# Eight blocks of each V gradient on ScalarE, six kept V tiles, four gradient tiles

## The chip, the cores and the metric

The kernel runs on one core of one Trainium2 chip. The metric is the device time of one execution in microseconds (us). Before the change it is 903.56 us, the median of 3 runs (903.27 to 903.65). The profile is one further execution of the same program. A measurement of this kernel agrees with its repetitions to within about 0.1%.

The engines are named as in the profile: PE is TensorE (PEld its weight loads), DVE is VectorE, ACT is ScalarE, POOL is GpSimd, SP is the engine that issues the loads. GB/s is what the core's 16 DMA engines moved.

## The reference

The reference computes one decoding step of a transformer block and all its gradients. With `B = 2` batch rows, `H = 32` heads, `Sk = 4096` cached positions and `Dh = 128`:

```
def _A_ref(x, k_cache, v_cache, wq, wo):
    q = (x @ wq) by heads
    scores = einsum("bhqd,bhkd->bhqk", q, k) * (Dh ** -0.5)
    p = _softmax(scores, axis=-1)
    o = einsum("bhqk,bhkd->bhqd", p, v)
    return o @ wo
def _B_ref(x, w1, w2):
    return relu(x @ w1) @ w2

h  = x + _A_ref(_layernorm(x), k_cache, v_cache, wq, wo)
h2 = h + _B_ref(_layernorm(h), w1, w2)
_out, _vjp = jax.vjp(_f, A_x, A_k_cache, A_v_cache, A_wq, A_wo, B_w1, B_w2)
_grads = _vjp(grad_out)
```

Almost all bytes are the K and V caches and their gradients. For each pair of batch row and head there are a K and a V tile of 4096 x 128 bf16 (1024 KB each) to read and a K and a V gradient of the same size to write. Each gradient is an outer product. Row s of the V gradient is `P[s]` (the softmax weight) times the vector `go` of that head. Row s of the K gradient is `gs[s]` times the query, with `gs[s] = P[s] * (V[s] . go - dot)`. So the gradient of K needs V a second time, once `go` is known, and `go` needs the whole forward pass of its batch row.

## The kernel before, in words

**Two sweeps.** The first sweep (`p1_iter`, one pass per pair, 64 pairs in order) reads K and V, makes scores, softmax and sums, and keeps the softmax weights in `P_bf`. The second sweep (`p2_iter`, one turn j per pair) reads V again (in the second sweep a V tile is called W), multiplies it with `go` and writes both gradients. The second sweep starts while the first still runs on batch row 1, one turn for two passes. From pass 64 on there is a turn in each, and after pass 65 the second sweep runs alone, from turn 14 to turn 63.

**Kept tiles.** The V tiles of the last `KEPT[b]` heads of a batch row stay in the on-chip memory after the first sweep, and the second sweep takes these heads first (`turns`), so they are not read again. `KEPT = (6, 5)`: six of batch row 0 and five of batch row 1, thus 53 W loads for 64 turns. The kept heads of batch row 1 are turns 32 to 36.

**Tiles and their homes.** Tiles of 1024 KB come from a list of homes (`take`, `give`). There are 12 at first, 14 when the second sweep runs alone, and more at the end. A home has a tag: `ld` for loads, `g` for gradients (`gK`, `gV`), `f` and `q` for late work. `share(ld=..., g=...)` says how many homes of each tag are wanted, and `give` moves a returned home to a tag that has too few. Homes of one tag are taken in the order in which they were given back. When the second sweep runs alone, line 1147 asks for `KEPT[1] + 4 = 9` load tiles and 5 gradient tiles. From turn `H + KEPT[1] - 1 = 36` on, line 1158 shares for the late work. Loads are issued on SP in one fixed order (`queue`, `pump`), each as soon as the order of the program has given a load home back, and SP waits there until the last user of that home is done.

**A turn.** `p2_iter` is a generator of six steps (a `yield` ends each):

- step 0: the last of four rounds of L436 for the head before (V times `go`), its `gsp` on VectorE (L821), `rb` on ScalarE (L835, the rows `go` and q of this head, spread over all partitions and scaled by one number per partition), `pp` on POOL (L837), the first of four transposes of W (TensorE L423, copied to `t_sb` by ScalarE, L428), and the first half of the K gradient of the head before (L808);
- step 1: the second half of that K gradient and its store, issued on POOL (L846);
- steps 2 to 4: the other three transposes with their copies, and the L436 rounds; step 4 also returns W and makes the first half of this head's V gradient (`gV`, L808);
- step 5: the second half of `gV`, and its store, issued on POOL (L865).

A half is one VectorE instruction on 128 x 2048 elements (`outer_half`). There are no barriers between steps: each engine works through its own list of instructions and waits only for what an instruction needs. Between the steps, other work is inserted at set rates: the middle of the network (`middle_gen`, whose L644 steps make `go` in groups of heads, first a group of the kept heads), the outer products for the weight gradients (`fin_gen`, tiles `ot`), and the gradient of x (`gx_gen`).

Of the kernel before, what the change touches and what calls it, by code (L numbers as in the profile page):

```python
# [7 lines left out]
FP32 = mybir.dt.float32  # L8
BF16 = mybir.dt.bfloat16
ALU = mybir.AluOpType  # L10
# [5 lines left out]
def kernel(  # L16
# [20 lines left out]
    nc = tc.nc  # L37
# [67 lines left out]
    def give(t, to=None):  # L105
        tag, k, _ = home_of.pop(id(t))
        to = to or goes_to(tag)
        owned[tag] -= 1
        owned[to] += 1
        free[to] += 1  # L110
        homes[to].append(k)
        given_at[k] = step[0]
# [279 lines left out]

    pairs = [(b, h) for b in range(B) for h in range(H)]
    NP1 = len(pairs)
    KEPT = (6, 5)
    turns = [(b, h) for b in range(B) for h in (*range(H - KEPT[b], H), *range(H - KEPT[b]))]
    turn_of = {bh: j for j, bh in enumerate(turns)}
    kept = {(b, h) for b in range(B) for h in range(H - KEPT[b], H)}
# [404 lines left out]
    def pairs_view(t):  # L803
        return t.rearrange("p s (a two) -> p s a two", two=2)

    def outer_half(dst, row, colp, k):
        sl = slice(k * HALF, (k + 1) * HALF)
        nc.vector.tensor_tensor(  # L808
            out=pairs_view(dst[:, sl, :]),
            in0=row.rearrange("p (a two) -> p a two", two=2)[:, None, :, :].to_broadcast([128, HALF, 64, 2]),  # L810
            in1=colp[:, sl, None, :].to_broadcast([128, HALF, 64, 2]), op=ALU.mult)

    def p2_iter(j, busy):

        c = S2[j] if j < NP1 else None
        p = S2[j - 1] if j >= 1 else None
# [7 lines left out]
        if c is not None:  # L824
            b, h = turns[j]
            go = gom[:, h, b, :, :]

            bank = pst([128, 512], FP32, "sps", "dp_ps")
            for k, col in enumerate((goc, qsc)):
                nc.tensor.matmul(bank[:, 128 + k * 128:256 + k * 128],  # L830
                                 lhsT=col[:, h, b:b + 1].to_broadcast([128, 128]), rhs=ident_bf[:],
                                 start=True, stop=True)
            c["dp"] = bank[:, 0:NSC]
            rb = mats.tile([128, 256], BF16, tag="rb", bufs=4, name="rb")
            nc.scalar.activation(out=rb[:], in_=bank[:, 128:384], func=ACT.Copy, scale=rt[:, b, h:h + 1])  # L835
            pp = small.tile([128, NSC, 2], BF16, tag="pp", name="pp")
            nc.gpsimd.tensor_copy(out=pp[:], in_=P_bf[:, b * H + h, :, None].to_broadcast([128, NSC, 2]))  # L837
            c.update(rb=rb, pp=pp)
            c["T0"] = pair_transpose(c["W"], 0, busy=busy)
        if p is not None:  # L840
            gK = take("g", [128, NSC, 128], "gK")
# [2 lines left out]
        if p is not None:  # L844
            outer_half(gK, p["rb"][:, 128:256], gsp, 1)
            nc.gpsimd.dma_start(out=natural(out_2, bp, hp), in_=gK[:])  # L846
            give(gK)
            del S2[j - 1]
        yield
        if c is None:  # L850
            return
        c["T1"] = pair_transpose(c["W"], 1, busy=busy)
        pair_matvec(c["dp"], c.pop("T0"), 0, go)
        yield
        c["T2"] = pair_transpose(c["W"], 2, busy=busy)
# [5 lines left out]
        gV = take("g", [128, NSC, 128], "gV")  # L861
        outer_half(gV, c["rb"][:, 0:128], c["pp"], 0)
        yield
        outer_half(gV, c["rb"][:, 0:128], c["pp"], 1)
        nc.gpsimd.dma_start(out=natural(out_3, b, h), in_=gV[:])  # L865
        give(gV)
        yield


# [270 lines left out]
    for n, (i, j) in enumerate(plan):  # L1140
        all_go = all(("go", B - 1, h) in done for h in range(H))
        if i is None and plan[n - 1][0] is not None:
            pkp.release()
            big1 = tc.alloc_tile_pool(name="big1", bufs=1)
            for _ in range(2):
                more_home("ld", big1)
            share(ld=KEPT[1] + 4, g=5)
        if all_go and not late[0]:
            wop.release()
            big3 = tc.alloc_tile_pool(name="big3", bufs=1, side="right")  # L1150
# [8 lines left out]
        if j is not None:  # L1159
            while g2 is not None:  # L1160
                p2_step()
            if j < NP1:
                bg_until(("go", *turns[j]))
            g2 = p2_iter(j, 0)
        if i is None and ("w1", 1) in done and fin is None:
            wts.release()
            fin = tc.alloc_tile_pool(name="fin", bufs=1)
# [90 lines left out]
```

## Time and profile before

| | |
|---|---|
| median of 3 runs | 903.56 us |
| the profiled execution | 902.98 us, of which the span from the first to the last instruction is 901.1 us |
| busy: PE, DVE, ACT, POOL | 82%, 77%, 49%, 21% of the span |
| read, written | 212.16 MB, 149.13 MB |
| a half of `gV` or `gK` on VectorE (128 x 2048) | 1.22 us |
| `rb` on ScalarE (128 x 256, scale per partition) | 0.474 us |
| a `t_sb` copy on ScalarE (128 x 512) | 0.587 us |
| `pp` on POOL (most of them) | 0.25 us |
| `gV` stores, issue to landing | 14.8 us median, 4.3 to 29.1 |

The span by stage, with the mean granted clock of TensorE and the rate of the DMA:

| stage, us | what runs | clock | GB/s |
|---|---|---|---|
| 0 to 222 | first sweep, batch row 0 | 0.97 | 402 |
| 222 to 311 | middle of the network for batch row 0 | 0.98 | 343 |
| 311 to 444 | first sweep, batch row 1, with the second sweep at half rate | 0.95 | 422 |
| 444 to 622 | end of the first sweep, then the second alone, turns to 32 | 0.62 | 411 |
| 622 to 735 | turns 33 to 45 with the late work | 0.58 | 404 |
| 735 to 888 | the other turns | 0.58 | 424 |
| 888 to 901 | the last stores land | 0.50 | 249 |

In the profile's tables a line of a stretch gives, after its bounds and length, the busy time of PE, PEld, DVE, ACT and POOL with the number of instructions, then the granted clock, the DMA share and GB/s. A line of a timeline gives start, duration, engine, source line and what is written from what. A line of waits gives the total, the number of times and the longest, in us.

### The profile page before, as it was taken

To read this page: it belongs to the slowest core of one execution; us is meant where nothing else is said; L and a number is where in the kernel's file an instruction comes from. 1 tells how busy PE (TensorE), PEld (TensorE's weight loads), DVE (VectorE), ACT (ScalarE), POOL (GpSimd) and SP (SyncE) were. 2 spreads that over 40 slices of the span, in tenths; PEclk is the share of its full clock that TensorE was granted. 3 is DMA by queue.
4 is the path that set the end of the run, shared out by engine and by line. 5 is a ranking of instruction groups with operands and counts; after the bars stand their busy time and mean duration, and the time that the engine had idled before them with its cause. 6 is when DMAs were issued, how large, how long until landed. Compare 5 with 4: busy or idle time off the path is not lost.

```text
span 901.1 us, 24395 instructions
## 1 busy us (share of the span) xinstructions
PE 739.2 (82%) x10145; PEld 618.0 (69%) x10145; DVE 695.8 (77%) x1284; ACT 442.9 (49%) x1090; POOL 192.9 (21%) x330
## 2 busy tenths in 40 slices
PE   4998899899999897997877856865887799679780
PEld 4887788788888786886766845653766576466460
DVE  2665778677779886886878879978897459999972
ACT  1443334344456564564543534543665666467560
POOL 1343434343311111010011112111221111111120
PEclk9999999899999999898995556655566555575565
DMA  9999999999789999999999999999999999999997
GB/s 377 419 409 405 409 397 409 419 419 359 301 323 341 415 423 422 421 423 422 417 384 403 421 424 395 423 418 416 415 417 406 408 379 424 425 425 425 425 423 319
DMA packets 56430, 362.87 MB, mean 403 GB/s; under 512 B 5696, under 2 KB 11776, under 8 KB 15488
## 3 DMA queue, kind: packets, MB, share of 16 engines
q1 hardware_dynamic: 34664, 212.17, 58.3%
q0 software_dynamic: 18432, 134.23, 35.7%
q10 hardware_dynamic: 3224, 14.92, 4.0%
q8 instruction: 80, 1.31, 0.6%
q14 instruction: 30, 0.25, 0.1%
HBM read 212.16 MB, written 149.13 MB: 401 GB/s over the span
## 4 chain that ended last, share of the span: by engine, by line
PE 47%; DMA 25%; DVE 15%; ACT 5%; issue 5%; SPq 0%; POOL 0%; ACTq 0%; POOLq 0%; DVEq 0%
PE t_ps L423 20%; DMA Vt<-in_A_v_cache_dram 12%; PE m_ps L457 10%; DMA out_dram<-gV 7%; DVE gV L808 5%; DMA out_dram<-gK 4%; PE s_ps L436 3%; DVE gK L808 3%; PE u_ps L486 3%; ACT t_sb L428 3%; PE o_ps L902 3%; PE dp_ps L436 2%; DVE pk L464 2%; DVE junk L644 2%; DMA Kt<-in_A_k_cache_dram 2%
## 5 line engine op out<-in xcount | busy, mean ns | idle before, releaser
L428 ACT COPY t_sb<-t_ps 128x512 f32<-128x512 f32 x479 | 274.4, 587 | 212.5 <-PE t_ps L423 206.3
L436 PEld LDWEIGHTS <-t_sb 128*128 128x128 bf16 x4096 | 179.3, 102 | 43.1 <-ACT t_sb L428 21.4
L423 PE MATMUL t_ps<-ident_f,Wt 128*128 128x128 f32 x848 | 196.4, 380 | 0.2 <-ACT t_sb L428 0.2
L457 PE MATMUL m_ps<-pk,Vt 128*128 128x129 bf16 x2048 | 173.5, 224 | 18.0 <-DMA Vt<-in_A_v_cache_dram 16.0
L464 DVE TENSOR_TENSOR pk<-Kt,ep 128x2048 bf16<-128x2048 bf16 x128 | 156.5, 1223 | 30.8 <-ACT ep L512 14.1
L808 DVE TENSOR_TENSOR gK<-rb,gsp 128x2048 bf16<-128x2048 bf16 x128 | 152.5, 1225 | 17.2 <-DMA out_dram<-gV 15.2
L423 PE MATMUL t_ps<-ident_f,Kt 128*128 128x128 f32 x1024 | 156.9, 287 | 6.7 <-DMA Kt<-in_A_k_cache_dram 6.2
L808 DVE TENSOR_TENSOR gV<-rb,pp 128x2048 bf16<-128x2048 bf16 x128 | 152.9, 1219 | 10.0 <-DMA out_dram<-gK 7.9
L457 PEld LDWEIGHTS <-Vt 128*128 128x128 bf16 x2048 | 126.7, 99 | 49.2 <-issue 29.8
L423 PEld LDWEIGHTS t_ps<-ident_f,Wt 128*128 128x128 f32 x848 | 137.2, 198 | 29.3 <-issue 23.4
L423 PEld LDWEIGHTS t_ps<-ident_f,Kt 128*128 128x128 f32 x1024 | 114.0, 146 | 11.0 <-issue 5.9
L474 POOL COPY pk<-ep 128x16 bf16<-128x16 bf16 x80 | 84.8, 1062 | 166.5 <-ACT ep L512 86.8
L436 PE MATMUL dp_ps<-gom,t_sb 128*128 128x2 bf16 x2048 | 95.8, 168 | 10.9 <-ACT t_sb L428 10.4
L846 POOL DMA_DIRECT2D out_dram<-gK x64 | 34.0, 532 | 267.3 <-DVE gK L808 204.8
L865 POOL DMA_DIRECT2D out_dram<-gV x64 | 34.2, 534 | 258.1 <-DVE gV L808 202.2
L436 PE MATMUL s_ps<-qm,t_sb 128*128 128x2 bf16 x2048 | 87.7, 164 | 1.5 <-DVE t_sb L426 1.5
L908 ACT CAST ot<-o_ps 128x512 bf16<-128x512 f32 (+3 forms) x152 | 67.2, 492 | 10.7 <-DMA out_dram<-ot 9.2
L571 ACT CAST MT<-m_ps 128x128 bf16<-128x128 f32 x64 | 17.1, 267 | 107.7 <-PE m_ps L457 107.6
L821 DVE SCALAR_TENSOR_TENSOR gsp<-dp_ps,negdot,P_bf 128x64 bf16<-128x64 f32 x64 | 18.0, 281 | 52.0 <-PE dp_ps L436 51.6
L835 ACT ACTIVATE rb<-dp_ps,rt 128x256 bf16<-128x256 f32 x64 | 30.4, 475 | 56.0 <-PE dp_ps L830 55.2
L644 DVE CUSTOM_DVE_ANT_0 junk<-wo_t,hbc 128x640 bf16<-128x640 bf16 x64 | 52.4, 819 | 0.2
L644 DVE CUSTOM_DVE_ANT_0 gxj<-wqs,gqr 128x1024 bf16<-128x1024 bf16 x40 | 48.8, 1221 | 0.2
(198 smaller groups left out, 702.7 us busy)
## 6 DMA issues: line engine op xcount, KB each, us to landing
Kt<-in_A_k_cache_dram SPq DMA_DIRECT2D x64, 1024.0 KB, 15.0
Vt<-in_A_v_cache_dram SPq DMA_DIRECT2D x64, 1024.0 KB, 13.8
out_dram<-gV POOLq DMA_DIRECT2D x64, 1024.0 KB, 14.8
out_dram<-gK POOLq DMA_DIRECT2D x64, 1024.0 KB, 14.1
Wt<-in_A_v_cache_dram SPq DMA_DIRECT2D x53, 1024.0 KB, 12.5
wq_t<-in_A_wq_dram SPq DMA_DIRECT2D x5, 1024.0 KB, 6.9
wo_t<-in_A_wo_dram SPq DMA_DIRECT2D x4, 1280.0 KB
wqs<-in_A_wq_dram SPq DMA_DIRECT2D x5, 1024.0 KB, 15.8
```

Of the source, the lines that this page charges most:

```text
L423: nc.tensor.transpose(t_ps[:, j, :], natf[:, 2 * cc:2 * cc + 2, :].rearrange("p c k -> p (c k)"), ident_f[:])
L428: nc.scalar.copy(out=t_sb[:], in_=t_ps[:])
L436: nc.tensor.matmul(dst[:, sc:sc + 2], lhsT=v[:, j, :, par], rhs=vecs[:, par, :], start=(par == 0), stop=(par == 1))
L457: nc.tensor.matmul(r["m"][:, 0:129], lhsT=r["V"][:, sc, :], rhs=r["pk"][sc // HALF][:, sc % HALF, 0:129], start=(sc == 0), stop=(sc == NSC ...
L464: nc.vector.tensor_tensor(out=p["pk"][k][:, :, 0:128].rearrange("p s (a two) -> p s a two", two=2), in0=p["K"][:, sl, :].rearrange("p s (a ...
L474: nc.gpsimd.tensor_copy(out=col, in_=e)
L644: nc.vector.tensor_tensor_reduce(out=junk[0:kc, 0:width], in0=in0, in1=in1, scale=1.0, scalar=0.0, op0=ALU.mult, op1=ALU.add, accum_out=acc)
L808: nc.vector.tensor_tensor(out=pairs_view(dst[:, sl, :]), in0=row.rearrange("p (a two) -> p a two", two=2)[:, None, :, :].to_broadcast([128 ...
L835: nc.scalar.activation(out=rb[:], in_=bank[:, 128:384], func=ACT.Copy, scale=rt[:, b, h:h + 1])
L846: nc.gpsimd.dma_start(out=natural(out_2, bp, hp), in_=gK[:])
L865: nc.gpsimd.dma_start(out=natural(out_3, b, h), in_=gV[:])
L908: nc.scalar.copy(out=ot[0:P, k, n0:n0 + nn], in_=o_ps[0:P, 0:nn])
```

## The change

Three things change together.

1. `KEPT` becomes (6, 6). A sixth V tile of batch row 1 stays. There are 52 W loads; the kept heads are turns 32 to 37; the first `go` group of batch row 1 has six heads and the last has two instead of three. `share` in line 1147 asks for `KEPT[1] + 4 = 10` load tiles, and the sharing for the late work begins one turn later.
2. In that same line the gradient tiles asked for are 4, not 5.
3. In turns 14 to 32 (the second sweep alone, `j <= H`) VectorE leaves out the last eight of the 32 blocks of each `gV` (a block is 128 x 128), so its second half is 128 x 1024. ScalarE makes these eight in step 2 of the next turn, behind the copy of that turn's second transpose: each is `rb` times one number per partition. POOL copies these numbers to fp32 (`pa`) in step 0. The store of `gV` is then issued in step 2 of the next turn, on POOL behind `pp`, `pa` and the K store, and the tile is returned only there.

```diff
-    KEPT = (6, 5)
+    KEPT = (6, 6)
...
-    def outer_half(dst, row, colp, k):
-        sl = slice(k * HALF, (k + 1) * HALF)
+    def outer_half(dst, row, colp, k, short=0):
+        n = HALF - short
+        sl = slice(k * HALF, k * HALF + n)
...
-    def p2_iter(j, busy):
+    def p2_iter(j, busy, act=0):
...
+            if act:
+                pa = small.tile([128, act], FP32, tag="pa", bufs=2, name="pa")
+                nc.gpsimd.tensor_copy(out=pa[:], in_=P_bf[:, b * H + h, NSC - act:NSC])
             c["T0"] = pair_transpose(c["W"], 0, busy=busy)
...
+        yield
+        if c is not None:
+            c["T1"] = pair_transpose(c["W"], 1, busy=busy)
+        if p is not None:
+            if "gV" in p:
+                gV, pa, bp, hp, n = p["gV"]
+                for k in range(n):
+                    nc.scalar.activation(out=gV[:, NSC - n + k, :], in_=p["rb"][:, 0:128], func=ACT.Copy,
+                                         scale=pa[:, k:k + 1])
+                nc.gpsimd.dma_start(out=natural(out_3, bp, hp), in_=gV[:])
+                give(gV)
             del S2[j - 1]
...
-        outer_half(gV, c["rb"][:, 0:128], c["pp"], 1)
-        nc.gpsimd.dma_start(out=natural(out_3, b, h), in_=gV[:])
-        give(gV)
+        outer_half(gV, c["rb"][:, 0:128], c["pp"], 1, act)
+        if act:
+            c["gV"] = (gV, pa, b, h, act)
+        else:
+            nc.gpsimd.dma_start(out=natural(out_3, b, h), in_=gV[:])
+            give(gV)
...
-            share(ld=KEPT[1] + 4, g=5)
+            share(ld=KEPT[1] + 4, g=4)
...
-            g2 = p2_iter(j, 0)
+            g2 = p2_iter(j, 0, 8 if i is None and j <= H else 0)
```

## The prediction

> **What bounds the kernel now.** I read the page's slices first, then the chain, then busy time by stretch, the load queue by time, the waits of VectorE and the stores' landing times.
>
> The page's slices of the span, and its chain by engine:
>
> ```profile
> DMA  9999999999789999999999999999999999999997
> GB/s 377 419 409 405 409 397 409 419 419 359 301 323 341 415 423 422 421 423 422 417 384 403 421 424 395 423 418 416 415 417 406 408 379 424 425 425 425 425 423 319
> PE 47%; DMA 25%; DVE 15%; ACT 5%; issue 5%; SPq 0%; POOL 0%; ACTq 0%; POOLq 0%; DVEq 0%
> ```
>
> The DMA engines are full in nearly every slice, at 415 to 425 GB/s where nothing disturbs them. TensorE leads the chain, but from slice 20 (450 us) on it is the DMA that is full while the others have gaps. Busy time by stretch (PE, weight loads, DVE, ACT, POOL, granted clock, DMA share, GB/s) shows the part that the change touches:
>
> ```profile
> 444.00:454.00 10.00, 7.88 (x111) 7.04 (x110) 6.63 (x18) 4.47 (x11) 0.53 (x1) 0.83 0.96 399
> 454.00:462.00 8.00, 7.29 (x134) 6.46 (x132) 6.89 (x12) 4.02 (x13) 2.02 (x3) 1.00 0.95 349
> 484.00:540.00 56.00, 43.82 (x502) 39.50 (x500) 47.66 (x83) 25.95 (x47) 10.13 (x23) 0.53 1.01 414
> 540.00:564.00 24.00, 15.05 (x179) 13.55 (x179) 23.52 (x42) 11.07 (x27) 4.93 (x10) 0.64 1.00 397
> 540.00:588.00 48.00, 34.48 (x373) 28.46 (x374) 46.22 (x83) 23.94 (x56) 9.63 (x21) 0.64 1.01 410
> 588.00:622.00 34.00, 27.09 (x236) 20.71 (x236) 27.16 (x47) 18.46 (x41) 5.39 (x10) 0.50 1.01 419
> ```
>
> Turns 14 to 32 lie in 484 to 622. The V stores of turns 14 and 32 are issued at 483.74 and 622.37 us, so one turn takes 138.6 / 18 = 7.70 us and moves one load and two stores, 3.15 MB. VectorE is 96% busy from 540 to 588 and less elsewhere; ScalarE stays at 46 to 54%. The load queue by time, at the end of the first sweep:
>
> ```profile
> 428.64 0.33 SPq L444 DMA_DIRECT2D Kt<-in_A_k_cache_dram  x1
> 429.06 0.60 SPq L444 DMA_DIRECT2D Vt<-in_A_v_cache_dram  x1
> 436.15 0.33 SPq L444 DMA_DIRECT2D Wt<-in_A_v_cache_dram  x1
> 437.34 0.33 SPq L444 DMA_DIRECT2D Vt<-in_A_v_cache_dram  x1
> 443.79 0.33 SPq L444 DMA_DIRECT2D Wt<-in_A_v_cache_dram  x1
> 454.02 0.33 SPq L444 DMA_DIRECT2D Vt<-in_A_v_cache_dram  x1
> ```
>
> Each issue waits for a tile that compute gives back. After 443.79 none is given back for 10 us, and that is where the stretch above falls to 399 and 349 GB/s. Next, what VectorE waited for in 484 to 622, and the K stores' time to landing in a stretch paced by the DMA and in one paced by VectorE:
>
> ```profile
> DVE gK L808 <- DMA out_dram<-gV: 8.9, 8, 1.9
> DVE gV L808 <- DMA out_dram<-gK: 4.2, 5, 1.7
> ```
> ```profile
> L846 POOL DMA_DIRECT2D out_dram<-gK x4: 531/531/533, 506.7 to 531.5; - x4
> ...
> DMA to landing us min/median/max: 14.1/17.8/19.0
> ```
> ```profile
> L846 POOL DMA_DIRECT2D out_dram<-gK x4: 531/531/531, 541.0 to 561.5; - x4
> ...
> DMA to landing us min/median/max: 9.5/11.3/12.9
> ```
>
> VectorE waits for gradient tiles, a little at a time. With landings of 17.8 us and about 8.5 us a turn, two stores a turn are 2 x 17.8 / 8.5 = 4.2 in flight: all five tiles but the one being filled. In 540 to 564 it is 2 x 10.5 / 6.9 = 3.0.
>
> **The change, part by part.**
>
> *The sixth kept V tile.* It drops one 1024 KB load of 53 W loads: 1.05 MB at the 424 GB/s of 735 to 888 us is 2.5 us of DMA time. But the tile is held from the sweep's turn 60, and each later load moves one give-back later: the V tile issued at 429.06 goes at 436.15, the W tile of 436.15 at 437.34, the V tile of 437.34 at 443.79, and the W tile of 443.79 at 454.02. Up to 443.79 earlier loads are still in service (the V tile of 429.06 landed at 446, when TensorE stops waiting for it), so nothing is lost. Then the DMA has 1.05 MB less to move before 454.02: 399 GB/s over 10 us becomes about (3.99 - 1.05) / 10 us = 294 GB/s. After 454 the two kernels have the same bytes to go. The saving is handed back in that gap: 0 us net. Bounds: -2.5 (the gap closes otherwise) and 0. What is late next is the last V tile, issued at 455.72 for 454.02 and wanted at 463.1; before it landed in 6.6 us, now it shares with the W tile ahead of it, 2.1 MB in 7.4 us, which is 283 GB/s and is met by the 349 of that stretch.
>
> *Four gradient tiles, and a store that leaves later.* Before, a V tile was filled by two halves (1.22 us each) and its store issued at once. Now its last eight blocks come from ScalarE in the next turn, and on the POOL queue its store stands behind `pp`, `pa` and the K store of the same turn. Its filling lasts 1.22 + 0.61 (the short half, by its size; at most 1.22) + 0.82 (one L644 step) + 0.28 (gsp) + 2.45 (two gK halves) + 0.5 (issue) = 5.9 us, against some 3 before; gK's is 2.75 as it was. At 7.7 us a turn four tiles give (4 x 7.7 - 8.65) / 7.7 = 2.9 in flight, against 4.3 for five. The nearest row is 540 to 564 with 3.0 in flight: 397 GB/s. The 18 turns are 56.6 MB, at 397 GB/s 142.6 us, +4.0. The wider row 540 to 588 has 410 GB/s: 138.1, -0.5. I take +3.0, nearer to the first because its in-flight count is the nearest; another end is in the rivals.
>
> The page "DMA: Bandwidth & Descriptors" of the Trainium skill (Queues, rings and completion order) says that each DMA engine takes turns between the queue rows that have work, a packet at a time. By that alone a load and two stores would keep every engine fed with four tiles as with five, and this term would be 0 and the sum 903.1; the 349 GB/s at 454, with two loads and two stores under way, is the row that speaks against leaning on it.
>
> *VectorE's relief.* One half of gV shrinks by 0.61 us in each of 19 turns, 11.6 us of VectorE. It counts only where VectorE sets the pace, 540 to 588, seven turns or 4.3 us; there the DMA has from 410 to 424 GB/s to give, 48 x 3.3% = 1.6 us. Bounds -1.6 and 0; I take -0.5, since fewer tiles act on the same stretch.
>
> *ScalarE's eight blocks.* No row shows them. Below: a 128x128 cast takes 0.27 us, 8 x 0.27 = 2.2 us. Above: the 128x256 `rb` with a scale per partition takes 0.474, 8 x 0.474 = 3.8. Taken off by the width (0.587 for 512 and 0.267 for 128, 0.83 ns an element), `rb` at 128 is 0.37: 2.9 us a turn. ScalarE has 25.95 / 56 x 7.7 = 3.6 us a turn from 484, 4.2 from 588: 6.5 to 7.1 of 7.7. Behind the blocks on its queue stand the third and fourth copy of `t_sb`; for these TensorE's L436 waits, and for that VectorE's gsp. The first block also waits until the store that last left its tile has landed, the same event for which VectorE's gV half waits. From there VectorE has gV, gsp, gK and the next gV to do, some 7 us, before it needs the fourth copy; ScalarE needs 2.9 + 2 x 0.59 and TensorE about 1. Cost 0; without that cover up to 3 us in all (a turn's excess of 0.2 us in 588 to 622, and one late start). The page "ScalarE: Activation LUTs" (What ACT_TABLE_LOAD costs) gives a trn2 ACTIVATE 186 ns and 0.833 ns an element, 93 ns more for a per-partition operand, and an overlap of 93 ns back to back. That is an estimate of 0.29 us a block and 2.3 us a turn, and the sum is the same by it.
>
> *POOL's 19 copies `pa`* are like `pp` at 0.25 us, on an engine that is under 20% busy: 0, at most 0.25 x 19 = 4.8 if each held a store, which the waits of POOL for VectorE (some 3 us before most stores) exclude.
>
> *Later turns.* The group of go vectors is six heads, then the last two and not three; the work is the same. The buffers for the final outer products and for wq come one turn later, and turns 37 to 41 issue no load, where 36 to 39 did before. In 622 to 735 the DMA runs at 404 GB/s, 5.4 us short of 424. Both kernels have the same tiles by turn 42. I take 0, between -2 and +2: less than half of that shortage either way.
>
> Sum: 0 + 3.0 - 0.5 + 0 + 0 + 0 = +2.5 us. The profiled execution took 902.98 us (span 901.1), the median of the runs 903.56; on its own time the sum gives 905.5, on the median 906.1.
>
> **The rivals.** (a) *Faster.* The saved 2.5 us stay saved and four tiles suffice. For it: landings of 9.5 us were seen, and 410 GB/s with few tiles. Against it: the 10 us without a give-back at 444. It decides if the tile of 454.02 comes 2.5 us earlier. 903.56 - 2.5 - 0.5 = 900.6. (b) *Slower by much.* The K store must land before the next turn's gV starts, and from there to the next K store are 5.7 us (the filling without the wait to issue), so two turns take landing + 5.7. With 9.5 us this is 7.6 us a turn and costs nothing; with 11.3, the median, it is 8.5. A landing of 10.5, midway, gives 8.1: 19 x 0.4 = 7.6 us, 911. For it: five tiles already make VectorE wait 13 times. Against: those landings had more stores ahead of them. It decides above 9.7 us. (c) *No change.* The gap takes the saving and nothing else moves: 903.6.
>
> **How the numbers follow.** My forecast, slower by a little, has a chance of 0.37 (own range 904 to 908.5); (a) 0.30; (b) 0.17; (c) 0.16. Range 900.3 to 911: it holds (a) and reaches to (b). About 0.2% (1.8 us) is what a measurement of this kernel can tell from none; of the forecast's 0.37, 0.10 lies within. Faster 0.30, same 0.10 + 0.16 = 0.26, slower 0.27 + 0.17 = 0.44.
>
> **What would show it.** One W load fewer, and 444 to 454 at about 294 GB/s: step one; at 399 it is wrong. Landings of gK at 9 to 10 us with 395 to 405 GB/s in turns 14 to 32: step two; 415 or more and rival (a) lives, 390 and less with landings over 10.5 is (b). VectorE's waits for landings above the 13.1 us of the two rows. A third `t_sb` copy that TensorE waits for would be the price on ScalarE. The prediction is wrong most easily by 622 to 735, where work of three queues moves by a turn.

## The result, and the profile after

The changed kernel takes 912.92 us (median of 6 runs, 909.09 to 916.08); the kernel before took 903.41 us beside it. The ratio is 1.0107, with a 95% interval of 1.0082 to 1.0132: +9.7 us, between +7.4 and +11.9. The forecast was 906.1 with a range to 911.0. Slower was right, the size was not. Single executions spread more than the three of the text ahead let one think: the kernel before, run beside the experiments, took 899.1 to 910.0 us, with medians of 902.85 to 904.53. A difference of medians under some 3 us is not clear of that.

The profiled execution took 914.56 us (span 912.8). The changed kernel's slices of the span, and its chain by engine:

```profile
DMA  9999999998789999999899999999999899999997
GB/s 377 427 416 418 418 409 418 425 410 348 279 313 367 409 397 424 425 424 425 350 393 417 416 420 364 365 421 394 386 414 386 353 393 423 424 426 424 424 424 311
PE 44%; DMA 20%; DVE 14%; issue 11%; ACT 8%; POOL 2%; SPq 1%; ACTq 0%; POOLq 0%; DVEq 0%
```

The first slices are not slower than before, some are faster (427 against 419, 416 against 409). From slice 24 to 32 (the 25th to 33rd figure) the rate drops again and again to 353 to 394. ScalarE's share of the chain grew from 5% to 8%, "issue" from 5% to 11%. Busy time by stretch of the changed kernel, with the columns as before (five engines, clock, DMA share, GB/s):

```profile
444.00:454.00 10.00, 8.30 (x101) 7.66 (x102) 5.35 (x11) 3.37 (x8) 0.53 (x1) 0.66 0.79 333
454.00:462.00 8.00, 7.30 (x141) 6.46 (x139) 6.89 (x11) 4.35 (x13) 2.02 (x3) 1.00 0.85 254
484.00:540.00 56.00, 41.51 (x485) 34.91 (x483) 42.10 (x79) 41.48 (x108) 14.27 (x28) 0.58 1.01 417
540.00:564.00 24.00, 13.87 (x133) 12.56 (x130) 19.36 (x36) 14.02 (x37) 5.99 (x12) 0.50 0.94 365
540.00:588.00 48.00, 33.62 (x312) 27.06 (x309) 37.79 (x72) 32.86 (x91) 11.82 (x24) 0.50 0.98 378
588.00:622.00 34.00, 26.44 (x253) 20.27 (x251) 25.85 (x50) 25.22 (x67) 7.82 (x17) 0.55 1.01 406
484.00:622.00 138.00, 101.57 (x1038) 82.24 (x1036) 105.73 (x199) 99.56 (x266) 33.91 (x68) 0.55 1.00 401
622.00:760.00 138.00, 105.39 (x991) 81.12 (x990) 94.45 (x150) 83.33 (x186) 21.72 (x46) 0.56 0.97 388
```

Before, 540 to 588 ran at 410 GB/s and the two long stretches at 414 and 408. The changed kernel lost 13 x 138 = 1.8 MB in 484 to 622 and 20 x 138 = 2.8 MB in 622 to 760, at 420 GB/s 4.3 and 6.6 us. These are stretches of fixed time, though, and the turns in them shift. Counted from one event of the program to the next, here the issue of the K stores of turns 13 and 32, first before and then after:

```profile
480.03 0.53 POOL L846 DMA_DIRECT2D out_dram<-gK  x1 [5.31 <-DVE h1c L734]
626.14 0.53 POOL L846 DMA_DIRECT2D out_dram<-gK  x1 [3.00 <-DVE gK L808]
```
```profile
480.22 0.53 POOL L850 DMA_DIRECT2D out_dram<-gK  x1 [5.49 <-DVE h1c L734]
633.36 0.53 POOL L850 DMA_DIRECT2D out_dram<-gK  x1 [5.31 <-DVE gK L809]
```

The spans differ by 11.7 us: 0.2 up to the first of these stores, 7.0 between the two and 4.5 from the second to the end. VectorE is idler than before (37.79 of 48 us in place of 46.22) and ScalarE busier. The load queue of the changed kernel at the end of the first sweep, and what VectorE waited for in 484 to 622 us (total, times, longest):

```profile
434.92 0.33 SPq L444 DMA_DIRECT2D Wt<-in_A_v_cache_dram  x1
441.37 0.33 SPq L444 DMA_DIRECT2D Vt<-in_A_v_cache_dram  x1
454.40 0.33 SPq L444 DMA_DIRECT2D Wt<-in_A_v_cache_dram  x1
456.10 0.33 SPq L444 DMA_DIRECT2D Vt<-in_A_v_cache_dram  x1
```
```profile
DVE gK L809 <- DMA out_dram<-gV: 14.4, 7, 2.9
DVE gV L809 <- DMA out_dram<-gK: 9.2, 5, 3.1
```

The gap is as forecast: no issue between 441.37 and 454.40, 333 GB/s in 444 to 454 and 254 after it. That fits a saved megabyte that is handed back, but does not show it by itself: several runs below with five kept tiles have 335 to 377 GB/s in 444 to 454. VectorE's waits for landings rose from 13.1 to 23.6 us. The K stores' time to landing in the changed kernel, in 500 to 540 and in 540 to 564 us:

```profile
L850 POOL DMA_DIRECT2D out_dram<-gK x5: 533/533/533, 504.4 to 535.2; - x5
DMA to landing us min/median/max: 7.9/9.1/9.7
...
L850 POOL DMA_DIRECT2D out_dram<-gK x3: 533/533/533, 542.7 to 556.8; - x3
DMA to landing us min/median/max: 7.2/8.3/9.1
```

Landings are shorter than before (17.8 and 11.3), not longer. Fewer stores are in flight: counted from issue to landing, 2.5 on average over 484 to 622, and 3.8 before. In 540 to 564 the DMA is not kept at work (share 0.94).

One more sign misled me at first. The page's group of weight loads for L436, in the changed kernel:

```profile
L436 PEld LDWEIGHTS <-t_sb 128*128 128x128 bf16 x4096 | 177.3, 102 | 72.7 <-ACT t_sb L428 42.5
```

Before it was 43.1 us of idle time, 21.4 of it for ScalarE's copies. The eight blocks stand between the second and the third copy, so the first theory was that they lengthen the chain from copy to L436 to `gsp` and so pace the turns.

### The profile page after: what moved, and what is told of

Read it like the earlier page. It is cut to its first block, busy times and chain, and to the rows that moved or that the text cites. A ratio compares the mean times of both kernels' runs of the same rounds, so it can differ in the third digit from the quotient of the medians.

```text
span 912.8 us, 24577 instructions
## 1 busy us (share of the span) xinstructions
PE 747.6 (82%) x10145; PEld 619.6 (68%) x10145; DVE 685.9 (75%) x1284; ACT 484.7 (53%) x1242; POOL 200.0 (22%) x349
## 4 chain that ended last, share of the span: by engine, by line
PE 44%; DMA 20%; DVE 14%; issue 11%; ACT 8%; POOL 2%; SPq 1%; ACTq 0%; POOLq 0%; DVEq 0%
PE t_ps L423 18%; DMA Vt<-in_A_v_cache_dram 13%; PE m_ps L457 10%; DVE gxj L644 3%; PE s_ps L436 3%; DVE gV L809 3%; DMA out_dram<-gV 3%; PE u_ps L486 3%; ACT t_sb L428 3%; DVE gK L809 3%; PE o_ps L918 3%; PE dp_ps L436 2%; ACT gV L859 2%; DMA Kt<-in_A_k_cache_dram 2%; DVE pk L464 2%
## 5 line engine op out<-in xcount | busy, mean ns | idle before, releaser
L436 PEld LDWEIGHTS <-t_sb 128*128 128x128 bf16 x4096 | 177.3, 102 | 72.7 <-ACT t_sb L428 42.5
L464 DVE TENSOR_TENSOR pk<-Kt,ep 128x2048 bf16<-128x2048 bf16 x128 | 156.4, 1223 | 34.5 <-PE m_ps L457 16.5
L809 DVE TENSOR_TENSOR gK<-rb,gsp 128x2048 bf16<-128x2048 bf16 x128 | 152.0, 1223 | 23.3 <-DMA out_dram<-gV 21.4
L457 PEld LDWEIGHTS <-Vt 128*128 128x128 bf16 x2048 | 126.7, 100 | 51.2 <-issue 29.7
L809 DVE TENSOR_TENSOR gV<-rb,pp 128x2048 bf16<-128x2048 bf16 (+1 forms) x128 | 143.1, 1142 | 17.0 <-DMA out_dram<-gK 9.2
L436 PE MATMUL dp_ps<-gom,t_sb 128*128 128x2 bf16 x2048 | 95.7, 168 | 27.4 <-ACT t_sb L428 26.2
L436 PE MATMUL s_ps<-qm,t_sb 128*128 128x2 bf16 x2048 | 87.6, 164 | 1.5 <-DVE t_sb L426 1.5
L881 POOL DMA_DIRECT2D out_dram<-gV x45 | 24.2, 537 | 198.8 <-DVE gV L809 157.4
## 6 DMA issues: line engine op xcount, KB each, us to landing
Kt<-in_A_k_cache_dram SPq DMA_DIRECT2D x64, 1024.0 KB, 14.4
out_dram<-gV POOLq DMA_DIRECT2D x64, 1024.0 KB, 11.7
```

Of the source, the lines that this page charges most:

```text
L436: nc.tensor.matmul(dst[:, sc:sc + 2], lhsT=v[:, j, :, par], rhs=vecs[:, par, :], start=(par == 0), stop=(par == 1))
L457: nc.tensor.matmul(r["m"][:, 0:129], lhsT=r["V"][:, sc, :], rhs=r["pk"][sc // HALF][:, sc % HALF, 0:129], start=(sc == 0), stop=(sc == NSC ...
L464: nc.vector.tensor_tensor(out=p["pk"][k][:, :, 0:128].rearrange("p s (a two) -> p s a two", two=2), in0=p["K"][:, sl, :].rearrange("p s (a ...
L809: nc.vector.tensor_tensor(out=pairs_view(dst[:, sl, :]), in0=row.rearrange("p (a two) -> p a two", two=2)[:, None, :, :].to_broadcast([128 ...
```

## The experiments

Deltas are ratios to the kernel before, run on the same chip beside it, times 903.5 us, with the 95% interval in brackets. Rates are of each run's profiled execution. Five theories were told apart: (1) ScalarE's blocks lengthen the chain; (2) four gradient tiles are too few; (3) the sixth kept tile moves later work; (4) the place of the large tiles in the on-chip memory; (5) the late store holds a tile too long. The last two were formed on the way.

**Blocks alone.** The change without its tile counts (diffs are against the changed kernel unless said otherwise):

```diff
-    KEPT = (6, 6)
+    KEPT = (6, 5)
...
-            share(ld=KEPT[1] + 4, g=4)
+            share(ld=KEPT[1] + 4, g=5)
```

> Blocks on ScalarE, the shortened half on VectorE and the late gV store alone: five kept V tiles and five gradient tiles as before the change. Theory 1 (ScalarE's blocks, 2.45 us between the second and the third copy, lengthen the chain copies - fourth round on TensorE - gsp - next copies that paces the turns from 16 on): +4 to +9 us, that is 907 to 912 us, and TensorE's wait for t_sb at line 436 stays at 60 to 75 us against 43.1 before. Theory 2 (four gradient tiles make VectorE wait for landings): 0 to +2 us. Theory 3 (the sixth kept tile moves late work, turns 33 to 34, 42 and 61 to 63): 0 to +1 us.

898.5 us, ratio 0.9947: -4.8 us [-6.9, -2.7]. Theory 1 falls at once, and nothing that I had predicted makes the kernel faster by 5 us.

**Six kept and four gradient tiles alone**, no blocks:

```diff
-            g2 = p2_iter(j, 0, 8 if i is None and j <= H else 0)
+            g2 = p2_iter(j, 0)
```

> Six kept V tiles and four gradient tiles, with no blocks on ScalarE: VectorE makes whole gV tiles and they are stored at once. Theory 1: -2 to +2 us, 901 to 906 us, TensorE's wait for t_sb at 40 to 48 us. Theories 2 and 3: +4 to +9 us, 907 to 912 us; theory 2 with VectorE's waits for landings above 22 us, theory 3 with the loss in turns 33 to 34 and 61 to 63.

911.31 us, ratio 1.0084: +7.6 us [4.7, 10.5].

**The late store without ScalarE**, whole tiles by VectorE:

```diff
-                for k in range(n):
-                    nc.scalar.activation(out=gV[:, NSC - n + k, :], in_=p["rb"][:, 0:128], func=ACT.Copy,
-                                         scale=pa[:, k:k + 1])
...
-        outer_half(gV, c["rb"][:, 0:128], c["pp"], 1, act)
+        outer_half(gV, c["rb"][:, 0:128], c["pp"], 1)
```

> The whole change, but VectorE makes the eight blocks too: the gV store still goes out in the next turn, behind that turn's second copy. Theory 1: 0 to +3 us, 903 to 907 us, nearly all of it from the tile that is held longer. Theory 2: +6 to +10 us, since four gradient tiles with one held longer give the most waits for landings. Theory 3: +4 to +9 us.

910.43 us, ratio 1.0065: +5.9 us [3.5, 8.2], without any block on ScalarE.

**ScalarE's time alone**, on five and five tiles. VectorE makes and stores whole `gV` tiles at once, and the blocks go to scratch:

```diff
...
-                    nc.scalar.activation(out=gV[:, NSC - n + k, :], in_=p["rb"][:, 0:128], func=ACT.Copy,
+                    nc.scalar.activation(out=u4[:].bitcast(BF16)[:, (k % 2) * 128:(k % 2) * 128 + 128], in_=p["rb"][:, 0:128], func=ACT.Copy,
                                          scale=pa[:, k:k + 1])
...
```

> The kernel before (five kept V tiles, five gradient tiles, VectorE makes and stores whole gV tiles at once), to which ScalarE's eight blocks a turn are added at the changed kernel's place, written to a scratch tile that nobody reads. The price of ScalarE's time alone. Theory 1: +5 to +9 us, 908 to 912 us. Theories 2 and 3: 0 to +1.5 us.

899.33 us, ratio 0.9953: -4.2 us [-6.1, -2.3]. A kernel that only does more work became faster. The time by turns said where: the thirteenth K store, issued before any block was made, came 6.8 us earlier in the blocks-alone run than in the kernel before, and 4.1 us earlier in this one. Common to the runs with a gain in the first stretch is one thing, the tile `pa`. Its two buffers of 32 bytes lie among the small tiles, ahead of the large ones. In the built programs the first large tile starts 192 bytes past a multiple of 256 before, and on a multiple of 256 with `pa`, and all the large tiles of that side move with it. That gave theory 4.

**64 unused bytes**, in the kernel before:

```diff
+    small.tile([128, 32], BF16, tag="pad", bufs=1, name="pad")
```

> The kernel before, with one unused tile of 64 bytes a partition among the small tiles, so that every large tile of the left side starts at a multiple of 256 bytes, as in the changed kernel, and not 192 bytes past one; no instruction differs. Theory 4 (the tile pa gained by moving the large tiles: the runs with it moved 420 to 422 GB/s at 20 to 60 and 140 to 180 us, those without 414): -3 to -5 us, 898 to 900 us, with the gain before 444 us. Rival (the gain of the first batch is the blocks' own, or ScalarE's extra work paces the turns well): -0.5 to +0.5 us.

**32 unused bytes**, which ends 224 past a multiple of 256:

```diff
+    small.tile([128, 16], BF16, tag="pad", bufs=1, name="pad")
```

> The kernel before with an unused tile of 32 bytes a partition instead of 64: the large tiles move by half as much and start 224 bytes past a multiple of 256, so still none on one. Theory 4 in its sharp form (what counts is a start on a multiple of 256 bytes): -1 to +1 us, 414 GB/s at 20 to 60 us as before. Rival (any move, or the new place of the small tiles, does it): -2 to -5 us and about 420 GB/s.

64 bytes: 898.3 us, ratio 0.9949, -4.6 us [-7.0, -2.3]. 32 bytes: 904.69 us, ratio 1.0017, +1.5 us [-0.4, 3.4]. The stretch 20 to 180 us, in which only loads run, in the kernel before:

```profile
20.00:180.00 160.00, 148.71 (x2467) 129.82 (x2467) 112.65 (x206) 63.45 (x190) 62.07 (x78) 0.96 1.02 410
```

with 32 bytes more:

```profile
20.00:180.00 160.00, 151.22 (x2482) 132.88 (x2481) 113.52 (x207) 64.14 (x191) 62.82 (x79) 0.98 1.02 409
```

and with 64:

```profile
20.00:180.00 160.00, 152.02 (x2565) 133.64 (x2565) 117.34 (x215) 65.41 (x196) 64.80 (x81) 0.99 1.02 418
```

The DMA share is the same 1.02; what it moves differs. The same split holds in every profile of this study: 409 or 410 GB/s where the large tiles start off a multiple of 256 bytes (seven profiles), 417 to 420 where they start on one (thirteen). 8 GB/s over 160 us is 1.3 MB, 3.1 of the 4.6 us; where the rest lies is not resolved. Only 0, 192 and 224 bytes past were run, so whether a multiple of 128 would do, or one of 512 is needed, is not shown. The page "DMA: Bandwidth & Descriptors" of the Trainium skill (How a descriptor splits into AXI transactions) says that a transaction reads up to 256 bytes and starts on a multiple of 256, so that bytes ahead of an unaligned start are fetched for nothing. It is worded for reading, and here the written side moved. If it holds there, a row of 8192 bytes at 192 past costs 262 beats of 32 bytes in place of 256, an estimate of 2.3%; the rows above show 2.0%. In the stretches with stores no such gain is seen (735 to 888 us ran at 424 GB/s before).

**Blocks alone at the old place**: the eight numbers lie in an old tile that is dead by then, so that no large tile moves.

```diff
...
-                pa = small.tile([128, act], FP32, tag="pa", bufs=2, name="pa")
+                pa = PA[0][:].bitcast(FP32)[:, j % 2 * act:j % 2 * act + act]
...
```

> Blocks, short half and late store alone, as in the first run, but the eight factors lie in an old tile that is dead by then, so that the large tiles stand where they stood before the change. Theory 4: -1 to +1 us against the kernel before, since the first run's -4.4 us was the place of the tiles; 414 GB/s at 20 to 60 us. Rival (the blocks' own gain): -3 to -5 us.

907.14 us, ratio 1.0035: +3.2 us [0.8, 5.5]. The gain is gone, as theory 4 has it. That it is worse than the kernel before was not expected; at the new place the same blocks stand at -4.8 against -4.6 for the 64 bytes, so with five and five tiles their own price is -0.2 there and +3.2 here. I leave it between.

**The whole change at the old place**, by the same edit:

> The whole change, but the eight factors lie in an old dead tile, so that the large tiles stay where they were before the change. Theory 4: the gain of the place is gone, +12 to +16 us against the kernel before (the change measured +9.5 with it). Rival (the place is worth nothing here, where the waits are others): +8 to +11 us.

915.86 us, ratio 1.0131: +11.8 us [9.2, 14.5], just under the expected band. Four pairs of runs differ by the place alone: 4.6 (nothing else changed), 8.0 (blocks alone), 2.1 (whole change; within the intervals) and, with the run below, 5.3 (six and four).

**Four gradient tiles alone**, and **six kept tiles alone**, both in the kernel before:

```diff
-            share(ld=KEPT[1] + 4, g=5)
+            share(ld=KEPT[1] + 5, g=4)
```

> Four gradient tiles instead of five (the fifth goes to the loads), everything else as before; five kept V tiles, large tiles at their old place. Theory 2 (four gradient tiles are what cost the 8.5 us of the second run): +6 to +9 us. Theory 3 (the sixth kept V tile costs it): 0 to +2 us. The prediction's own term for it was +3.0.

```diff
-    KEPT = (6, 5)
+    KEPT = (6, 6)
...
-            share(ld=KEPT[1] + 4, g=5)
+            share(ld=KEPT[1] + 3, g=5)
```

> Six kept V tiles instead of five with five gradient tiles (one tile less for the loads), everything else as before, large tiles at their old place. Theory 2: -1 to +2 us. Theory 3: +6 to +9 us. The prediction's own term was 0, between -2.5 and 0.

Four gradient tiles: 907.1 us, ratio 1.0049, +4.4 us [2.1, 6.8]. Six kept: 906.8 us, ratio 1.0038, +3.4 us [1.3, 5.6]. Neither theory 2 nor 3 is the whole; together they are 7.8, and both at once measured 7.6. Where each loses is told by the K stores of turns 13 and 32, and not by the rate in a fixed stretch. With four gradient tiles alone, then with six kept tiles alone:

```profile
478.70 0.53 POOL L850 DMA_DIRECT2D out_dram<-gK  x1 [7.61 <-DVE h1c L734]
630.22 0.53 POOL L850 DMA_DIRECT2D out_dram<-gK  x1 [3.76 <-DVE gK L809]
```
```profile
476.98 0.53 POOL L850 DMA_DIRECT2D out_dram<-gK  x1 [6.26 <-DVE h1c L734]
622.00 0.53 POOL L850 DMA_DIRECT2D out_dram<-gK  x1 [2.56 <-DVE gK L809]
```

The same for all profiles with five or six kept tiles, those of the runs below included (one execution each; "wait" is what VectorE waited in 484 to 622 us for landings, us):

| tiles and store of `gV` | profiles | stores 13 to 32 | 32 to the end | wait |
|---|---|---|---|---|
| five kept, five gradient, at once | before, 64 and 32 bytes, scratch, both sides | 144.8 to 146.5 | 275.0 to 276.3 | 1.8 to 15.0 |
| five kept, four gradient, at once | four alone | 151.5 | 274.7 | 17.7 |
| six kept, five gradient, at once | six alone | 145.0 | 280.4 | 13.5 |
| six kept, four gradient, at once | without and with 64 bytes, scratch, blocks at once | 148.2 to 152.7 | 276.6 to 281.1 | 14.7 to 17.5 |
| six kept, four gradient, late | the change, at the old place, late store | 152.9 to 156.4 | 277.6 to 280.2 | 20.8 to 23.6 |
| five kept, five gradient, late | blocks alone, at the old place, late store | 145.8 to 151.9 | 274.7 to 277.3 | 7.3 to 15.7 |
| six kept, five gradient, late | the change with five | 145.7 | 281.3 | 12.6 |

Four gradient tiles cost 5 us between stores 13 and 32 and nothing behind them; from turn 36 or 37 on the program asks for five again. Six kept tiles cost nothing up to store 32 and 5 us behind it, nearly 4 of them in two turns: stores 32 to 34 take 19.8 us, with five kept tiles 15.7 to 18.0. So theory 2 loses where the prediction had put its term, and theory 3 where its expectation had put it, in turns 33 and 34. The rates of the fixed stretches mislead here:

```profile
484.00:622.00 138.00, 104.33 (x1085) 88.50 (x1085) 116.67 (x202) 66.18 (x139) 22.86 (x52) 0.55 0.99 410
622.00:760.00 138.00, 107.75 (x1048) 83.16 (x1046) 100.58 (x156) 82.23 (x179) 25.30 (x49) 0.57 0.98 395
```

These are four gradient tiles alone; before it was 414 and 408. That reads as if the price were paid behind 622. But the run has one load tile more, and at store 32 it has issued 33 W loads against 32 before: the bytes of the first stretch are partly loads that run ahead, and they are missing from the second.

**Six and four at the new place**: the second run with the 64 unused bytes, as base for those that follow.

```diff
+    small.tile([128, 32], BF16, tag="pad", bufs=1, name="pad")
...
-            g2 = p2_iter(j, 0, 8 if i is None and j <= H else 0)
+            g2 = p2_iter(j, 0)
```

> Six kept V tiles and four gradient tiles, no blocks and no late store, with the unused 64 bytes: the base on which the changed kernel's blocks and late store stand. Theory 4 and the sum of parts: +2.0 to +4.5 us (+7.6 for the two parts, -4.6 for the place). What is then left to the changed kernel, 5 to 7 us, is the price of the late store and of ScalarE's blocks with four tiles; if this run is at +7 us or more, these two are free.

906.87 us, ratio 1.0026: +2.3 us [0.2, 4.5]. So the blocks and the late store cost the changed kernel 9.7 - 2.3 = 7.4 us on six and four tiles, and nothing on five and five at this place (-4.8 against -4.6).

**ScalarE's time alone on six and four tiles**: the scratch run with the changed kernel's tile counts (diff against that run).

```diff
-    KEPT = (6, 5)
+    KEPT = (6, 6)
...
-            share(ld=KEPT[1] + 4, g=5)
+            share(ld=KEPT[1] + 4, g=4)
```

> Six kept V tiles and four gradient tiles with the large tiles at their new place; VectorE makes whole gV tiles, stored at once, and ScalarE makes the eight blocks as well, into a scratch tile that nobody reads. Against the run with six and four and 64 unused bytes (+2.4 us over the kernel before), this adds ScalarE's time alone. If ScalarE's chain is what cost the rest in the changed kernel (theory 1, with four tiles only): +5 to +8 us over the kernel before. If it is the later store of gV (a gradient tile held longer, theory 5): +1.5 to +4 us.

**The late store alone on five and five tiles**: the third run with the tile counts of the kernel before (diff against the third run).

```diff
-    KEPT = (6, 6)
+    KEPT = (6, 5)
...
-            share(ld=KEPT[1] + 4, g=4)
+            share(ld=KEPT[1] + 4, g=5)
```

> The late gV store alone, on five kept V tiles and five gradient tiles, large tiles at their new place; VectorE makes whole tiles. Theory 5 says that the hold costs only where no gradient tile is to spare: -5 to -3.5 us against the kernel before, as the 64 bytes alone (-4.6). If a tile held longer costs by itself: -2 to +1 us.

ScalarE's time alone: 903.03 us, ratio 0.9994, -0.5 us [-2.8, 1.6]: below both expectations, and no more than its base. The late store with a tile to spare: 900.12 us, ratio 0.9959, -3.7 us [-6.0, -1.5], 0.9 us from the 64 bytes alone. Theory 1 falls with four tiles as it did with five, and the page of the first of these runs shows why the sign was misleading:

```profile
L436 PEld LDWEIGHTS <-t_sb 128*128 128x128 bf16 x4096 | 177.9, 102 | 69.4 <-ACT t_sb L428 39.0
```

TensorE's wait for ScalarE's copies is nearly that of the changed kernel, and the median is ten microseconds lower (the profiled execution, at 908.69 us, is the slowest of its runs, so its rates are not used here).

**The blocks in the same turn, stored at once.** All else as in the change:

```diff
-            if "gV" in p:
...
-                give(gV)
...
-        if act:
-            c["gV"] = (gV, pa, b, h, act)
-        else:
-            nc.gpsimd.dma_start(out=natural(out_3, b, h), in_=gV[:])
-            give(gV)
+        for k in range(act):
+            nc.scalar.activation(out=gV[:, NSC - act + k, :], in_=c["rb"][:, 0:128], func=ACT.Copy,
+                                 scale=pa[:, k:k + 1])
+        nc.gpsimd.dma_start(out=natural(out_3, b, h), in_=gV[:])
+        give(gV)
```

> The whole change, but ScalarE makes its eight blocks in the same turn, behind that turn's fourth copy, and the gV store goes out at once instead of in the next turn; six kept V tiles, four gradient tiles, VectorE's half as short as in the change. Theory 5 (the tile held longer by the late store is what cost the changed kernel some 7 us over its base of six and four): -1 to +4 us against the kernel before. If the blocks themselves, in whatever place, cost it with four tiles: +7 to +10 us, as the change.

**The whole change with five gradient tiles**, the fifth taken from the loads:

```diff
-            share(ld=KEPT[1] + 4, g=4)
+            share(ld=KEPT[1] + 3, g=5)
```

> The whole change with five gradient tiles instead of four, the fifth taken from the loads (six kept, three others): blocks and late store as in the change. Theory 5 (a tile held longer costs nothing where a gradient tile is to spare): -3 to +1 us, the sixth kept tile's +3.4 less the 4.6 of the place. If the six kept tiles are what makes the late store dear: +4 to +9 us.

At once: 903.66 us, ratio 1.0000 [0.9986, 1.0013]. Five gradient tiles: 902.44 us, ratio 0.9980, -1.8 us [-3.6, 0.1]. Either way the 10 us are gone: it takes the four tiles, and it takes the blocks and their store in the next turn. The first of the two runs moves the blocks on ScalarE's queue as well as the store, so it does not tell these apart. The late store without blocks stands at +5.9, 3.6 over the base of six and four, and the change 3.8 over that; by the intervals of the runs each step is uncertain by some 3 us. On the POOL queue, the changed kernel:

```profile
565.92 0.53 POOL L850 DMA_DIRECT2D out_dram<-gK  x1 [4.09 <-DVE gK L809]
568.11 0.53 POOL L861 DMA_DIRECT2D out_dram<-gV  x1 [1.66 <-ACT gV L859]
```

and the one that stores at once:

```profile
563.86 0.53 POOL L850 DMA_DIRECT2D out_dram<-gK  x1 [0.25 <-DVE gK L809]
569.05 0.53 POOL L874 DMA_DIRECT2D out_dram<-gV  x1 [4.66 <-ACT gV L872]
```

In the changed kernel the store behind a K store is that of the head before the one being worked on, made a turn ago. From the end of VectorE's part of `gV` to the issue of its store there are 5.7 us (median of turns 14 to 32), in the run that stores at once 2.0, in the six-and-four base 0.3. The stretch of turns 14 to 32, first of the run that stores at once, then of the late store with VectorE's whole tiles:

```profile
484.00:622.00 138.00, 102.30 (x1043) 84.57 (x1043) 110.08 (x197) 100.89 (x275) 41.17 (x71) 0.54 1.01 413
```
```profile
484.00:622.00 138.00, 92.27 (x1039) 76.83 (x1037) 112.01 (x197) 62.29 (x130) 34.34 (x68) 0.61 0.98 395
```

413 against 401 in the changed kernel and 395 here. The rates alone do not carry the point, since the first of these executions is the fastest of its runs (898.43 us, median 903.66) and the late store with five tiles has 407 in its profile. VectorE's waits for landings do: 20.8 to 23.6 us in the three runs with four gradient tiles and a late store, and no more than 17.7 in any other (table above). In the base of six and four they are these two, where the changed kernel had 14.4 and 9.2:

```profile
DVE gK L810 <- DMA out_dram<-gK: 12.8, 10, 2.2
DVE gV L810 <- DMA out_dram<-gV: 4.7, 4, 1.4
```

**The tile counts the other way.** The kernel before with the 64 bytes and four kept tiles; the freed tile goes to the gradients, then to the loads:

```diff
-    KEPT = (6, 5)
+    KEPT = (6, 4)
...
-            share(ld=KEPT[1] + 4, g=5)
+            share(ld=KEPT[1] + 4, g=6)
```

> The other way round: four kept V tiles of the second batch (one MB more to read, 2.5 us of traffic at 420 GB/s) and six gradient tiles, with the 64 unused bytes. If the price of the missing gradient tile goes on in this direction and the kept tile costs what it holds: -9 to -6 us against the kernel before. If five are enough: -4 to -1 us (the 64 bytes less the MB read).

```diff
-    KEPT = (6, 5)
+    KEPT = (6, 4)
...
-            share(ld=KEPT[1] + 4, g=5)
+            share(ld=KEPT[1] + 5, g=5)
```

> Four kept V tiles of the second batch, five gradient tiles and so one tile more for the loads that are not kept, with the 64 unused bytes. If the sixth kept tile cost 3.4 us because it took a tile from the loads, the step back gives -8 to -5 us against the kernel before; if that price was the sixth tile's alone and the fifth was right: -4 to -1 us.

900.42 us, ratio 0.9948, -4.7 us [-7.5, -1.9], and 899.67 us, ratio 0.9945, -5.0 us [-6.7, -3.3], against -4.6 for the 64 bytes: the first between the two expectations, the second at the edge of the better one. One megabyte more to read costs nothing, since 622 to 760 runs at 417 and 419 GB/s in place of 404. So from four to five kept tiles the time is flat within the intervals, whichever use gets the tile, and from five to six it rises.

**Both sides on multiples of 256 bytes**, in the kernel before. The tiles of the right side, among them `wo_t`, still started 224 past one:

```diff
+    edge = tc.alloc_tile_pool(name="edge", bufs=1, side="right")
+    edge.tile([128, 112], BF16, name="edge_t")
...
-        zero = small.tile([128, H * B], BF16, tag="zero", bufs=1, name="zero")
+        zero = small.tile([128, H * B], BF16, tag="pp", name="zero")
...
-            gxo = small.tile([128, ND], BF16, tag="gxo", bufs=2, name="gxo")
+            gxo = small.tile([128, ND], BF16, tag="nb", name="gxo")
```

> The kernel before with the large tiles of both sides on multiples of 256 bytes (two small tiles share older ones, 224 unused bytes on the right side): five kept V tiles, five gradient tiles, no blocks. Theory 4: a little better than the 64 bytes alone, -4.5 to -6.5 us against the kernel before, since the right side holds the output projection and some twenty tiles of the last turns. Rival: as the 64 bytes alone, -4 us, or less.

897.69 us, ratio 0.9926: -6.7 us [-9.3, -4.1], the fastest of the study, ahead of both kernels. That it also beats the 64 bytes alone (by 2.1 us) is within the intervals and not shown.

## Why the prediction was wrong

By the medians the +9.7 us are the place of the large tiles (-4.6), six kept and four gradient tiles (+7.6; the two together 3.0, measured 2.3 in one kernel), and the blocks with their late store on these tiles (+7.4). How the 7.4 divides is not shown: by way of the late store it is 3.6 and 3.8, by way of the blocks stored at once -2.3 and 9.7. By the turns of the profiled executions it is +0.2, +7.0 and +4.5 us up to store 13, up to store 32 and behind it, where the forecast had 0, +2.5 and 0.

*The sixth kept tile, "0 us net".* The gap at 444 came as described (333 GB/s there and 254 behind it, where 294 were forecast for the first), and between stores 13 and 32 the run of it alone loses nothing: 145.0 us, 146.1 before. Its price did not end there. That run costs 3.4 us, outside the bounds of -2.5 and 0.

*"Later turns", taken as 0, between -2 and +2.* This is the step that failed there. From store 32 to the end the run with six kept tiles alone takes 280.4 us in place of 275.0, the changed kernel 279.5. I had named 622 to 735 the stretch by which the prediction is most easily wrong, and then given it no price.

*"Four gradient tiles, and a store that leaves later", +3.0.* This is the other step that failed, and here it is the size. The place was right, and so were the signs: landings of 9.1 and 8.3 us and 401 GB/s, where 9 to 10 and 395 to 405 were forecast. From store 14 to store 32, before and after:

```profile
487.60:626.10 138.50, 102.17 (x1088) 85.72 (x1086) 121.14 (x211) 67.20 (x143) 25.41 (x54) 0.56 1.01 416
487.40:633.40 146.00, 107.89 (x1076) 86.72 (x1077) 112.15 (x211) 104.82 (x282) 35.35 (x72) 0.53 1.00 398
```

It is 7.5 us. My sum set one load and two stores a turn, 56.6 MB, against 138.6 us. The turns moved 138.5 us x 416 GB/s = 57.6 MB, and at my own 397 GB/s that is 145.1 us, +6.6 and not +4.0; then I took less, for the 410 of a wider row. Four tiles alone cost 4.4 us [2.1, 6.8]. The rule of the page "DMA: Bandwidth & Descriptors" of the Trainium skill (Queues, rings and completion order), that an engine takes turns between the rows that have work, had given 0 for this term; the run decides against reading it as "four tiles do as well as five".

*The filling time, 5.9 us.* A part of the same term, and too short. From the start of `gV`'s first half to the issue of its store the changed kernel takes 7.7 us (median of turns 14 to 32), the run that stores at once 3.8, the base of six and four 2.7. My count in flight, (4 x 7.7 - 8.65) / 7.7 = 2.9, becomes (4 x 7.7 - 7.7 - 2.75) / 7.7 = 2.6; the trace has 2.5 over 484 to 622, the base 3.1, and the kernel before 3.8 where I had 4.3. The stretch 540 to 564, with its share of 0.94 and 365 GB/s, is not the late store's: four gradient tiles alone have 350 there, and six and four stored at once 363 and 340. Rival (b) had the sign and nearly the size, by the wrong road: landings did not grow to 10.5 us, they shrank to 9.1 and 8.3. The wait for landings rose from 13.1 to 23.6 us all the same; that it is because each tile begins its journey later fits the waits of the table and is not shown apart from the blocks.

*"ScalarE's eight blocks, cost 0".* Right for ScalarE's time: -0.5 us for the scratch run with six and four tiles (its base +2.3), -4.2 with five and five (its base -4.6). Whether the blocks cost something where they complete a tile that is held is open (the 3.8 us above). The third copy that TensorE waits for, which I had called the price on ScalarE, was there (72.7 us of idle weight loads in place of 43.1), and in the scratch runs it cost nothing. Eight blocks in a row took 2.45 us, not 2.9; the estimate by the page "ScalarE: Activation LUTs" of the Trainium skill (What ACT_TABLE_LOAD costs), 2.3 us, was nearer than mine from the rows. One such row, from the changed kernel's timeline:

```profile
565.37 2.45 ACT L859 ACTIVATE gV<-rb,pa 128x128 bf16<-128x128 bf16 x8
```

*"VectorE's relief", -0.5.* Not measured by itself. VectorE's busy time fell by 9.9 us (695.84 to 685.94), and the run that stores at once is 2.3 us under its base; the scratch run, which has no relief, is 2.8 under it. So nothing speaks for more than the 0.5.

*"POOL's 19 copies `pa`", 0.* The copies cost nothing that was seen. The tile they write is as large as the 64 unused bytes that gave -4.6 us by where they pushed the others, and no term of mine looked there.

Left open: what takes the 5 us behind store 32 with six kept tiles (the runs show only the turns), why the blocks at the old place cost 3.2 us and at the new one nothing, and 1.5 of the 4.6 us of the place.

## What to carry to other kernels

Count a shared buffer from the first write to the landing, not from the issue: the same blocks and late store, which hold a tile some 5 us longer, stand at +9.7 us with four gradient tiles and at -1.8 with five. Price a change of tile counts in every stage that draws on the same tiles, above all the one with the most users. Compare two kernels from one event of the program to the next; a rate in a fixed stretch of time also counts the loads that run ahead. And when a change adds or resizes even a small tile, look up where the large ones come to lie; a control with the same bytes left unused costs one run.

## What the runs showed of the hardware

Where a large tile starts in the on-chip memory changed the rate of the loads into it: in 20 to 180 us, where only loads run, 417 to 420 GB/s on a multiple of 256 bytes and 409 or 410 at 192 or 224 past one, with the DMA busy at the same share. 64 bytes of unused space gave 4.6 us; with 32, which end 224 past, the kernel was no faster (+1.5 [-0.4, 3.4]). And a wait of TensorE for ScalarE that grows can be free: with the blocks into scratch the idle time of the page's group is 59.9 us against 43.2 with the 64 bytes alone (five and five tiles) and 69.4 against 51.2 (six and four), and neither run is slower than its base clear of the noise (-4.2 against -4.6 us, -0.5 against +2.3).
